# The second expert's two input products as 2x2 blocks by seven products, its gated features kept in float32, and one turned output product

## The chip, the cores and the metric

The kernel runs on one core of a Trainium2 chip. The metric is the device time of one execution in microseconds (us). Four compute engines matter: PE (TensorE: matmuls, with a separate weight-load stream shown as PEld), DVE (VectorE), ACT (ScalarE) and POOL (GpSimd); SP (SyncE) issues the transfers.

## What is computed

```python
def reference(q, k, v, moe_w_in, moe_w_out, moe2_w_a, moe2_w_b, moe2_w_out):
    attn = softmax(causal(q @ k.T / 8)) @ v      # 2 batches, 12 heads, 448 tokens, 64
    x = attn                                     # as 896 tokens x 768
    h = x @ moe_w_in                             # 768 x 2048: the first expert
    y = (h - tanh(h)) @ moe_w_out                # 2048 x 768
    a, b = y @ moe2_w_a, y @ moe2_w_b            # 768 x 1536 each: the second expert
    return (a * b) @ moe2_w_out                  # 1536 x 768
```

## The kernel before

**Precision.** Each float32 operand of a product is split into a high and a low float32r part (names `xh`/`xl`, `wh`/`wl`, `gwh`/`gwl`: a trailing h is the high, l the low part). A product of one 128-deep block is then three matmuls (high by high, high by low, low by high), written by `matmuls` and `product` (lines 208 to 219).

**Weights.** A weight tile is 128 partitions x 768 (six 128x128 blocks; 640 where five are used). Five steps bring it in, each behind the other: `load_part` (two transfers on SP), `magnitude` (ACT, line 150), `bits` (DVE, line 162: tile `t`), `split_high` (ACT, line 173: `wh`) and `split_low` (DVE, line 184: `wl`; POOL during attention). `advance` calls each step once. How far each may run ahead is limited by counters: three raw tiles, TP = 2 tiles `t`, and a ring of seven pairs `wh`, `wl`, whose slots come free as products finish (`at["done"]`).

**Stages.** Attention goes first, in an order written out by hand (`ORDER`), with pieces of the first expert's first group as filler. Then come the three groups of the first expert (5, 6 and 5 feature blocks): `hidden` makes a block's features, and six output products (`dm` 0 to 5) add into `part` in SBUF (line 549); in the last group each sum is split into `yh`, `yl` (called `xh`, `xl` in rows; lines 553 and 554). The second expert has two groups of six feature blocks (`GROUPS2`). A block takes, for each of two pieces of tokens (512 and 384), 18 matmuls by `w_a` and 18 by `w_b`; ACT copies the one result (line 576), DVE multiplies it with the other (line 577), and `halve_g` splits the gated block (lines 466 and 467). After each group come 7 token tiles x 2 halves of an output product, 18 matmuls of 384 columns each; the second group adds to `opart` on DVE (line 599) and stores.

**Order.** Outside attention a scheduler orders each engine's instructions; each engine then works its list strictly in that order. Eight PSUM banks (`s` four, `t` two, `o` and `h` one each) are taken in turn by `next_bank`; a bank holds one product from its first to its last matmul, is read once or twice, and goes to the next product.

## Time and profile before

| | |
|---|---|
| median of 3 runs | 594.86 us (593.68 to 595.03) |
| the profiled execution, time | 593.73 us |
| the profiled execution, span from first to last instruction | 592.0 us |
| PE busy | 584.5 us, 99% of the span |
| DVE busy | 286.8 us, 48% |
| ACT busy | 276.1 us, 47% |
| POOL busy | 75.8 us, 13% |
| HBM read | 61.63 MB |

Busy PE time counts overlapping matmuls, so 99% says only that PE is hardly ever without work. How fast it goes is read from the starts of its matmuls. All durations come from the one profiled execution; its time lies 1.73 us over its span, and the median of the runs lies 1.13 us over its time.

### The profile page before, as it was taken

The numbers are of one execution on the slowest core, as the hardware profiler recorded it, in microseconds if no ns is written. First come the engines' busy times: TensorE is split into PE (matmuls) and PEld (weight loads), VectorE is DVE, ScalarE is ACT, GpSimd is POOL, SyncE is SP. The second block draws the span as 40 slices with busy tenths as digits, with TensorE's granted clock in tenths as the row PEclk, the third lists the DMA queues.
The fourth block names the chain that finished last, engine by engine and source line by source line (L and its number), as shares of the span: only waits on it lengthen the run. The fifth ranks groups of instructions, "written<-read, shape, count | busy, mean of one in ns | idle before, by whom it ended". The sixth has DMA issues, their size and how long they took to land.

```text
span 592.0 us, 8779 instructions
## 1 busy us (share of the span) xinstructions
PE 584.5 (99%) x3386; PEld 519.8 (88%) x3386; DVE 286.8 (48%) x552; ACT 276.1 (47%) x543; POOL 75.8 (13%) x93
## 2 busy tenths in 40 slices
PE   8999999999999999999999999999999999999997
PEld 4777887889988888888988999999999888889997
DVE  5788776427545554445567344444101754442111
ACT  5999888427565542235554333333312753321000
POOL 5788583300000000000000000000000000000000
PEclk9999999999999999999999999999999999999999
DMA  7645442217553332223343333333300843300111
GB/s 224 167 120 157 133 120 90 90 54 221 182 183 107 106 99 90 95 96 111 107 151 107 106 108 106 108 107 106 107 1 0 276 153 115 97 0 2 65 55 66
DMA packets 71114, 64.95 MB, mean 110 GB/s; under 512 B 13984, under 2 KB 71072, under 8 KB 71072
## 3 DMA queue, kind: packets, MB, share of 16 engines
q1 hardware_dynamic: 71072, 64.40, 34.8%
q8 instruction: 26, 0.43, 0.3%
q14 instruction: 16, 0.13, 0.1%
HBM read 61.63 MB, written 2.75 MB: 109 GB/s over the span
## 4 chain that ended last, share of the span: by engine, by line
PE 93%; ACT 5%; DVE 1%; issue 0%; POOL 0%; ACTq 0%; DVEq 0%
PE s L213 42%; PE t L213 19%; PE h L213 13%; PE o L213 9%; ACT p L323 3%; PE o L363 3%; PE t L337 2%; PE s L302 2%; PE h L435 1%; ACT pt L345 1%; PE t L382 0%; DVE p L314 0%; DVE t L162 0%; PE h L337 0%; ACT y L390 0%
## 5 line engine op out<-in xcount | busy, mean ns | idle before, releaser
L150 ACT CAST top<-raw 128x768 f16<-128x768 bf16 (+1 forms) x70 | 73.4, 1049 | 63.6 <-DVE t L162 31.4
L184 DVE TENSOR_TENSOR wl<-t,wh 128x768 fp32r<-128x768 f32 (+1 forms) x63 | 58.8, 936 | 88.3 <-ACT wh L173 86.3
L173 ACT CAST wh<-t 128x768 fp32r<-128x768 f32 (+1 forms) x70 | 56.9, 817 | 79.8 <-PE t L213 32.2
L213 PE MATMUL s<-xh,wl 128*128 128x512 f32 (+2 forms) x222 | 82.7, 373 | 0.0
L213 PE MATMUL s<-xl,wh 128*128 128x512 f32 (+2 forms) x222 | 82.6, 372 | 0.0
L213 PE MATMUL s<-xh,wh 128*128 128x512 f32 (+2 forms) x222 | 82.2, 370 | 0.0
L162 DVE SCALAR_TENSOR_TENSOR t<-raw,top 128x768 int32<-128x768 int32 (+1 forms) x70 | 68.2, 977 | 7.4 <-ACT top L150 5.6
L323 ACT ACTIVATE p<-p,m 112x448 f32<-112x448 f32 (+3 forms) x96 | 49.8, 525 | 6.3 <-DVE m L314 6.3
L213 PEld LDWEIGHTS s<-xl,wh 128*128 128x128 f32 x222 | 41.7, 188 | 5.6
L213 PEld LDWEIGHTS s<-xh,wl 128*128 128x128 f32 x222 | 41.6, 188 | 5.6
L213 PEld LDWEIGHTS s<-xh,wh 128*128 128x128 f32 x222 | 41.7, 188 | 5.6
L314 DVE CUSTOM_DVE_ANT_0 p<-s,mask 112x448 f32<-112x448 f32 (+3 forms) x96 | 37.7, 441 | 7.4 <-PE s L302 6.9
L213 PE MATMUL t<-xh,wl 128*128 128x384 f32 (+2 forms) x114 | 40.3, 354 | 0.0
L213 PE MATMUL t<-xh,wh 128*128 128x384 f32 (+2 forms) x114 | 40.3, 354 | 0.0
L213 PE MATMUL t<-xl,wh 128*128 128x384 f32 (+2 forms) x114 | 40.3, 353 | 0.0
L466 ACT CAST gwh<-e 128x512 fp32r<-128x512 f32 (+1 forms) x24 | 13.5, 563 | 38.8 <-DVE e L577 38.8
L213 PE MATMUL h<-xl,wh 128*128 128x448 f32 (+2 forms) x84 | 31.5, 375 | 0.0
L213 PE MATMUL h<-xh,wh 128*128 128x448 f32 (+2 forms) x84 | 31.3, 372 | 0.0
L213 PE MATMUL h<-xh,wl 128*128 128x448 f32 (+2 forms) x84 | 31.1, 370 | 0.0
L337 PE MATMUL t<-ident,p 112*112 112x112 f32 x202 | 29.6, 265 | 1.2 <-ACT pt L345 0.6
L337 PEld LDWEIGHTS t<-ident,p 112*112 112x112 f32 x202 | 21.3, 133 | 8.2 <-ACT pt L345 2.3
L213 PE MATMUL s<-wh,gwh 128*128 128x384 f32 x84 | 28.1, 334 | 0.0
(144 smaller groups left out, 1241.8 us busy)
## 6 DMA issues: line engine op xcount, KB each, us to landing
raw<-in_moe_w_out SPq DMA_DIRECT2D x48, 383.2 KB, 3.9
raw<-in_moe_w_in SPq DMA_DIRECT2D x32, 383.2 KB, 4.1
raw<-in_moe_w_a SPq DMA_DIRECT2D x24, 383.2 KB, 4.0
raw<-in_moe_w_b SPq DMA_DIRECT2D x24, 383.2 KB, 4.0
raw<-in_moe_w_out SPq DMA_DIRECT2D x12, 255.5 KB, 3.6
qk<-in_q SPq DMA_DIRECT2D x12, 224.0 KB, 2.8
qk<-in_k SPq DMA_DIRECT2D x12, 224.0 KB, 3.7
v<-in_v SPq DMA_DIRECT2D x24, 112.0 KB, 3.0
```

The lines of the kernel that those rows point to most:

```text
L150: nc.scalar.copy(out=tops[i % len(tops)][:, 0:nk, :, 1], in_=top[:, :, :, 2])
L162: nc.vector.scalar_tensor_tensor(out=ts[i], in0=low[:, :, :, 0], scalar=13, in1=top, op0=ALU.logical_shift_right, op1=ALU.bitwise_or)
L173: nc.scalar.copy(out=halves[i][0][:, 0:nk], in_=ts[i].bitcast(F32))
L184: engine.tensor_tensor(out=lo[:, 0:nk], in0=t.bitcast(F32), in1=hi[:, 0:nk].bitcast(F32), op=ALU.subtract)
L213: nc.tensor.matmul(o, a, b_, start=j == 0, stop=j == n - 1)
L302: nc.tensor.matmul(sc[i, c][e], a[r, 0, cs], b_[r, 1, :n], start=x == 0, stop=x == len(terms) - 1)
L314: nc.vector.tensor_tensor_reduce(out=p[:, e], in0=s, in1=mask[:QC, S - n:], scale=-scale, scalar=3.0e38, op0=ALU.add, op1=ALU.min, accum_o ...
L323: nc.scalar.activation(out=p[:, e], in_=p[:, e], func=ACTF.Exp, bias=least[i][:, c, e:e + 1], scale=-1.0, accum_out=sums[i][:, c, e:e + 1],)
L337: nc.tensor.transpose(out=pst[:QC, x * QC:(x + 1) * QC], in_=blk, identity=ident[:QC, :QC])
L345: nc.scalar.copy(out=out_, in_=in_)
L363: nc.tensor.matmul(o[64 * e:64 * e + 64, cs], vt[:, k_, e, :], p.rearrange("s c q -> s (c q)"), start=k_ == 0, stop=k_ == 2 * h + 1, skip_ ...
L466: nc.scalar.copy(out=hi, in_=gg)
```

## The change

The second expert's input products are made in **units**: one unit is one of the two weight matrices by two neighbouring feature blocks, so there are 12. The unit's operands are cut into 2x2 blocks (the 768-deep sum in halves of three blocks; two batches of 448 tokens; two feature blocks), and Strassen's scheme in Winograd's form gives the four results by seven products in place of eight. A product is nine matmuls of 448 columns. Its number m is 1 to 7; `turns` lists (unit, m).

- **Operands.** `y_terms` makes sums and differences of the first expert's output (lines 566 to 589 of the changed kernel) in the last output products, which now go in the order 0, 3, 1, 4, 2, 5 and in two pieces of 448. The extra operands `ext` and `ext4` take slots named `gwh`, `gwl`. `combine` makes four differences of weights for each unit on DVE (lines 188 to 194), in place in `t` or in `s3`. Weights are split half a tile at a time (384 columns), two halves to a ring slot; the ring has five slots instead of seven, `t` four instead of two.
- **Results.** Products 1, 6, 7 and 4 of a unit go one after another into one bank (X), 5 and 3 into a second (Z), 2 into a third (Y). `go_on` lets a product add to what the bank holds after it was read. ACT copies X after 1 and after 6 and Z after 5 (line 690); DVE adds Y to the first copy, X after 7 and Z after 3 to the others (line 664); ACT or DVE reads X once more after 4. DVE multiplies the results of the two matrices into `g32` (line 674).
- **Output.** The gated features stay in float32 until `split_g` splits all 12 blocks (lines 561 and 562), the first during the last unit, the others behind it. The output product then sums over all 12 blocks in one PSUM group: 6 row blocks x pieces of 512 and 384 tokens, 36 matmuls each, weights as the stationary operand; ACT copies the sum (line 725) and it is stored. The output is turned, and the host turns it back.

```diff
-    GROUPS2 = [6, 6]
-    TP = 2
+    DM_ORDER = (0, 3, 1, 4, 2, 5)
+    NF2 = DFF2 // 128
+    TP = 4
+    PARTS = 7
+    WB = 5
...
-    ep = ctx.enter_context(tc.tile_pool(name="e", bufs=2))
+    ep = ctx.enter_context(tc.tile_pool(name="e", bufs=8))
+    s3p = ctx.enter_context(tc.tile_pool(name="s3", bufs=2))
...
+    plan = [(i, None) for i in range(len(tiles))]
+    NU = NF2
+    base = len(tiles)
+    for f in range(0, NF2, 2):
+        for w in (w_a, w_b):
+            tiles += [block(w, slice(0, DM), f), block(w, slice(0, DM), f + 1)]
+    turns = []
+    for u in range(NU):
+        if u == 0:
+            turns += [(0, 1), (0, 5), (1, 1), (1, 5), (0, 2), (0, 6), (0, 7), (0, 3), (1, 2), (0, 4)]
+        elif u == 1:
+            turns += [(1, 6), (1, 7), (1, 3), (2, 1), (1, 4)]
+        elif u < NU - 1:
+            turns += [(u, 2), (u, 6), (u, 5), (u, 7), (u, 3), (u + 1, 1), (u, 4)]
+        else:
+            turns += [(u, 2), (u, 5), (u, 6), (u, 3), (u, 7), (u, 4)]
+    plan += turns
+    for dm in range(KD):
+        for h in range(2):
+            plan.append((len(tiles), None))
+            tiles.append(block(w_o, slice(h * DM, (h + 1) * DM), dm))
...
-        if i >= at["abs"] or i >= at["halve"] + TP:
+        while at["t"] in last_use and last_use[at["t"]] < at["halve"]:
+            at["t"] += 1
+        if i >= at["abs"] or i >= at["t"] + TP:
...
+    def source(j):
+
+        i, m = plan[j]
+        if m is None:
+            return ts[i].bitcast(F32)
+        if m == 7:
+            return thirds[i]
+        t = ts[base + 2 * i + int(m in (4, 5))].bitcast(F32)
+        return t[:, 3:6] if m in (2, 3, 4) else t[:, 0:3]
+
+    def combine(u, m):
+
+        t0, t1 = [ts[base + 2 * u + x].bitcast(F32) for x in range(2)]
+        a11, a12, a21, a22 = t0[:, 0:3], t0[:, 3:6], t1[:, 0:3], t1[:, 3:6]
+        if m == 3:
+            nc.vector.tensor_tensor(out=a12, in0=a12, in1=a11, op=ALU.subtract)
+        elif u not in summed:
+            summed.add(u)
+            thirds[u] = s3p.tile([128, 3, 128], F32, tag="s3", name="s3")
+            nc.vector.tensor_tensor(out=thirds[u], in0=a11, in1=a21, op=ALU.subtract)
+            nc.vector.tensor_tensor(out=a21, in0=a21, in1=a22, op=ALU.add)
+            nc.vector.tensor_tensor(out=a11, in0=a21, in1=a11, op=ALU.subtract)
+
     def split_high():
-        i = at["high"]
-        if i >= at["bits"] or i >= at["done"] + len(w_r.turns):
-            return
-        nk = ts[i].shape[1]
-        halves[i] = w_r.tile([([128, KD, 128], F32R, "wh"), ([128, KD, 128], F32R, "wl")])
-        nc.scalar.copy(out=halves[i][0][:, 0:nk], in_=ts[i].bitcast(F32))
+        j = at["high"]
+        if j >= len(plan) or j > at["halve"]:
+            return
+        i, m = plan[j]
+        full = m is None
+        if (i if full else base + 2 * i + int(m not in (1, 2))) >= at["bits"]:
+            return
+        if full or at["slots"] % 2 == 0:
+            if at["slots"] // 2 >= at["done"] // 2 + WB:
+                return
+            at["pair"] = [w_p.tile([128, KD, 128], F32R, tag=x, name=x) for x in ("wh", "wl")]
+        if m in (3, 5, 6, 7):
+            combine(i, m)
+        x = source(j)
+        nk = x.shape[1]
+        k0 = 0 if full else 3 * (at["slots"] % 2)
+        halves[j] = [t[:, k0:k0 + nk] for t in at["pair"]]
+        at["slots"] += 2 if full else 1
...
+                    o, a, b_, start=j == 0 and not go_on, stop=j == n - 1, skip_group_check=True
...
+    def y_terms(dm, b):
+
+        cs = BATCHES[b]
+        y = part[dm]
+        if b == 0:
+            yh[dm], yl[dm] = [xp.tile([128, NT], F32R, tag=x, name=x) for x in ("xh", "xl")]
+        if dm >= KD // 2 or b == 0:
+            halve(yh[dm][:, cs], yl[dm][:, cs], y[:, cs])
+        if b == 0:
+            return
+        if dm < KD // 2:
+            nc.vector.tensor_tensor(out=y[:, B0], in0=y[:, B1], in1=y[:, B0], op=ALU.subtract)
+            halve(yh[dm][:, B1], yl[dm][:, B1], y[:, B0])
+            return
+        kk = dm - KD // 2
+        t = part[kk]
+        ext[kk] = [g_full[0].tile([128, NT], F32R, tag=x, name=x) for x in ("gwh", "gwl")]
+        nc.vector.tensor_tensor(out=t[:, B0], in0=y[:, B1], in1=t[:, B0], op=ALU.subtract)
+        nc.vector.tensor_tensor(out=t[:, B1], in0=y[:, B1], in1=t[:, B1], op=ALU.subtract)
+        halve(*ext[kk], t)
+        nc.vector.tensor_tensor(out=y[:, B0], in0=y[:, B0], in1=t[:, B0], op=ALU.subtract)
+        if kk % 2 == 0:
+            ext4[kk // 2] = [g_full[0].tile([128, NT], F32R, tag=x, name=x) for x in ("gwh", "gwl")]
+        halve(*[x[:, BATCHES[kk % 2]] for x in ext4[kk // 2]], y[:, B0])
...
-    NTILE = NT // 128
-    NH = DM // 2
...
-            for cs in PIECES:
-                res = []
-                n = cs.stop - cs.start
-                for wh, wl in ws:
-                    o = next_bank()[:, :n]
-                    product(o, [((wh[:, kk], wl[:, kk]), (yh[kk][:, cs], yl[kk][:, cs])) for kk in range(KD)])
-                    res.append(o)
-                aa = ep.tile([128, 512], F32, tag="e0", name="e0")[:, :n]
-                ab = ep.tile([128, 512], F32, tag="e1", name="e1")[:, :n]
-                nc.scalar.copy(out=aa, in_=res[0])
-                nc.vector.tensor_tensor(out=ab, in0=res[1], in1=aa, op=ALU.mult)
-                halve_g(ab, gw[f][0][:, cs], gw[f][1][:, cs])
...
-            for hf in range(2):
-                o = next_bank()[:, :NH]
-                hs = slice(hf * 3, hf * 3 + 3)
-                product(
-                    o,
-                    [((gw[f][0][:, cs], gw[f][1][:, cs]), (ws[f][0][:, hs], ws[f][1][:, hs])) for f in range(g)],
-                )
-                dst = opart[t][:, hf * NH:(hf + 1) * NH]
-                if gi == 0:
-                    nc.scalar.copy(out=dst, in_=o)
-                else:
-                    nc.vector.tensor_tensor(out=dst, in0=o, in1=dst, op=ALU.add)
-                    nc.sync.dma_start(out=out[cs, hf * NH:(hf + 1) * NH], in_=dst)
...
+    def operand(m):
+        out = []
+        for kk in range(NK):
+            if m in (1, 5, 2, 3):
+                t = yh, yl
+                k, b = kk + NK * (m in (2, 3)), m in (5, 3)
+            elif m in (6, 7):
+                t = [{kk: ext[kk][x]} for x in range(2)]
+                k, b = kk, m == 7
+            else:
+                t = [{kk: ext4[kk // 2][x]} for x in range(2)]
+                k, b = kk, kk % 2
+            out.append([x[k][:, BATCHES[b]] for x in t])
+        return out
...
+    def split_g(f):
+
+        pool, tags = (g_full[0], ("gwh", "gwl")) if f == 0 or f > KD else (xp, ("xh", "xl"))
+        gs[f] = [pool.tile([128, NT], F32R, tag=x, name=x) for x in tags]
+        for b, cs in enumerate(BATCHES):
+            halve(*[x[:, cs] for x in gs[f]], g32[f][b])
...
+    def add(x, o):
+        nc.vector.tensor_tensor(out=x, in0=o, in1=x, op=ALU.add)
+
+    def outcome(u, q, x):
+
+        f, b = u // 2 * 2 + q // 2, q % 2
+        if u % 2 == 0:
+            left[q] = x
+            return
+        if f not in g32:
+            new_g32(f)
+        nc.vector.tensor_tensor(out=g32[f][b], in0=x, in1=left.pop(q), op=ALU.mult)
+
+    def turn(u, m):
+
+        wh, wl = next_weights()
+        parts = [((wh[:, kk], wl[:, kk]), b_) for kk, b_ in enumerate(operand(m))]
+        if m == 1:
+            X[u] = next_bank()[:, :S]
+        if m == 2:
+            Y[u] = next_bank()[:, :S]
+        if m == 5:
+            Z[u] = next_bank()[:, :S]
+        o = {1: X, 6: X, 7: X, 4: X, 2: Y, 5: Z, 3: Z}[m][u]
+        product(o, parts, go_on=m in (6, 7, 4, 3))
+        if m in (1, 6, 5):
+            c = {1: c1, 6: c2, 5: z}[m][u] = etile()
+            nc.scalar.copy(out=c, in_=o)
+        elif m == 2:
+            add(c1[u], o)
+            outcome(u, 0, c1.pop(u))
+        elif m == 7:
+            add(z[u], o)
+            outcome(u, 3, z.pop(u))
+        elif m == 3:
+            add(c2[u], o)
+            outcome(u, 1, c2.pop(u))
+        elif u % 2 == 0:
+            c = etile()
+            nc.scalar.copy(out=c, in_=o)
+            outcome(u, 2, c)
+        else:
+            outcome(u, 2, o)
+        at["done"] += 1
+        advance()
+
+    for u, m in turns:
+        if (u, m) == (NU - 1, 2):
+            split_g(0)
+        turn(u, m)
+    for f in range(1, NF2):
+        split_g(f)
+    for dm in range(KD):
+        ws = [next_weights() for _ in range(2)]
+        for cs in PIECES:
+            n = cs.stop - cs.start
+            o = next_bank()[:, :n]
+            product(
+                o,
+                [((ws[f // KD][0][:, f % KD], ws[f // KD][1][:, f % KD]), [x[:, cs] for x in gs[f]]) for f in range(NF2)],
+            )
+            r = ep.tile([128, 512], F32, tag="e", name="e")[:, :n]
+            nc.scalar.copy(out=r, in_=o)
+            nc.sync.dma_start(out=out[dm * 128:(dm + 1) * 128, cs], in_=r)
...
```

How this stands in each engine's list is shown at three places. **PE in the second expert's input stage**, before: the end of one product and the start of the next (`s_3676` and `t_3630` are banks, `xh_`, `xl_` the split output of the first expert, `wh_`, `wl_` weights).

```order
L213 MATMUL t_3630<-xh_3481,wh_3305 128x384
L213 MATMUL t_3630<-xl_3482,wh_3305 128x384
L213 MATMUL t_3630<-xh_3481,wl_3306 128x384
L213 MATMUL t_3630<-xh_3531,wh_3305 128x384
L213 MATMUL t_3630<-xl_3532,wh_3305 128x384
L213 MATMUL t_3630<-xh_3531,wl_3306 128x384
L213 MATMUL s_3676<-xh_3281,wh_3355 128x512
L213 MATMUL s_3676<-xl_3282,wh_3355 128x512
L213 MATMUL s_3676<-xh_3281,wl_3356 128x512
L213 MATMUL s_3676<-xh_3331,wh_3355 128x512
L213 MATMUL s_3676<-xl_3332,wh_3355 128x512
L213 MATMUL s_3676<-xh_3331,wl_3356 128x512
```

The same place now: `s_4103` is bank Z of one unit in its product 5, `h_3917` bank X of the unit ahead, which gets its product 7 here (`gwh_3351` and the like are `ext`).

```order
L251 MATMUL s_4103<-xl_3384,wh_3949 128x448
L251 MATMUL s_4103<-xh_3383,wl_3950 128x448
L251 MATMUL s_4103<-xh_3493,wh_3949 128x448
L251 MATMUL s_4103<-xl_3494,wh_3949 128x448
L251 MATMUL s_4103<-xh_3493,wl_3950 128x448
L251 MATMUL h_3917<-gwh_3351,wh_3852 128x448
L251 MATMUL h_3917<-gwl_3352,wh_3852 128x448
L251 MATMUL h_3917<-gwh_3351,wl_3853 128x448
L251 MATMUL h_3917<-gwh_3463,wh_3852 128x448
L251 MATMUL h_3917<-gwl_3464,wh_3852 128x448
L251 MATMUL h_3917<-gwh_3463,wl_3853 128x448
L251 MATMUL h_3917<-gwh_3566,wh_3852 128x448
```

A bank that was read after product 6 is written again, with another unit's product in between. **DVE in the same stage**, before: `e1` is the gated block, `gwl` its low part, `t` and `wl` the next weights.

```order
L577 TENSOR_TENSOR e1_3605<-h_3585,e0_3604 128x512
L467 TENSOR_TENSOR gwl_3565<-e1_3605,gwh_3564 128x512
L184 TENSOR_TENSOR wl_3656<-t_3509,wh_3655 128x768
L162 SCALAR_TENSOR_TENSOR t_3659<-raw_3461,top1_81 128x768
L577 TENSOR_TENSOR e1_3650<-t_3630,e0_3649 128x384
L184 TENSOR_TENSOR wl_3666<-t_3559,wh_3665 128x768
L162 SCALAR_TENSOR_TENSOR t_3669<-raw_3511,top0_80 128x768
L467 TENSOR_TENSOR gwl_3565<-e1_3650,gwh_3564 128x384
L577 TENSOR_TENSOR e1_3715<-o_3695,e0_3714 128x512
L467 TENSOR_TENSOR gwl_3675<-e1_3715,gwh_3674 128x512
L184 TENSOR_TENSOR wl_3766<-t_3659,wh_3765 128x768
L162 SCALAR_TENSOR_TENSOR t_3769<-raw_3561,top1_81 128x768
```

Now, in steady state (L192, L193, L194 and L188 are `combine`, L224 weight halves, L168 `bits`, L664 the additions, L674 the multiplications):

```order
L192 TENSOR_TENSOR s3_4069<-t_3912,t_3932 128x384
L193 TENSOR_TENSOR t_3932<-t_3932 128x384
L224 TENSOR_TENSOR wl_3984<-s3_3951,wh_3983 128x384
L224 TENSOR_TENSOR wl_3984<-t_3797,wh_3983 128x384
L168 SCALAR_TENSOR_TENSOR t_4031<-raw_3821,top0_83 128x768
L664 TENSOR_TENSOR e_4046<-o_4075,e_4046 128x448
L664 TENSOR_TENSOR e_3997<-h_3917,e_3997 128x448
L224 TENSOR_TENSOR wl_4015<-t_3912,wh_4014 128x384
L674 TENSOR_TENSOR g32_4012<-e_3997,e_3879 128x448
L224 TENSOR_TENSOR wl_4015<-t_3819,wh_4014 128x384
L194 TENSOR_TENSOR t_3912<-t_3932,t_3912 128x384
L664 TENSOR_TENSOR e_3981<-t_3987,e_3981 128x448
```

The instructions are shorter and more of them stand between two readings of a bank. **DVE in the last output products of the first expert**, before: `ypart` is the sum, `xl` its low part.

```order
L549 TENSOR_TENSOR ypart_1995<-s_3264,ypart_1995 128x512
L554 TENSOR_TENSOR xl_3282<-ypart_1995,xh_3281 128x512
L549 TENSOR_TENSOR ypart_1995<-o_3286,ypart_1995 128x384
L184 TENSOR_TENSOR wl_3306<-t_3197,wh_3305 128x768
L554 TENSOR_TENSOR xl_3282<-ypart_1995,xh_3281 128x384
L549 TENSOR_TENSOR ypart_2050<-s_3314,ypart_2050 128x512
L162 SCALAR_TENSOR_TENSOR t_3309<-raw_3137,top1_81 128x768
L554 TENSOR_TENSOR xl_3332<-ypart_2050,xh_3331 128x512
L549 TENSOR_TENSOR ypart_2050<-t_3336,ypart_2050 128x384
L184 TENSOR_TENSOR wl_3356<-t_3259,wh_3355 128x768
L554 TENSOR_TENSOR xl_3332<-ypart_2050,xh_3331 128x384
L162 SCALAR_TENSOR_TENSOR t_3359<-raw_3199,top0_80 128x768
```

The same place now; L577, L583 and L584 are the differences of `y_terms`.

```order
L619 TENSOR_TENSOR ypart_1998<-s_3259,ypart_1998 128x448
L562 TENSOR_TENSOR xl_3277<-ypart_1998,xh_3276 128x448
L619 TENSOR_TENSOR ypart_1998<-o_3281,ypart_1998 128x448
L224 TENSOR_TENSOR wl_3302<-t_3068,wh_3301 128x640
L577 TENSOR_TENSOR ypart_1998<-ypart_1998 128x448
L619 TENSOR_TENSOR ypart_2151<-s_3310,ypart_2151 128x448
L168 SCALAR_TENSOR_TENSOR t_3305<-raw_3132,top1_84 128x768
L562 TENSOR_TENSOR xl_3277<-ypart_1998,xh_3276 128x448
L562 TENSOR_TENSOR xl_3328<-ypart_2151,xh_3327 128x448
L192 TENSOR_TENSOR s3_3438<-t_3254,t_3305 128x384
L619 TENSOR_TENSOR ypart_2151<-t_3332,ypart_2151 128x448
L224 TENSOR_TENSOR wl_3363<-t_3130,wh_3362 128x384
```

Differences, weight differences and weight halves now stand between the additions.

## Rows read from the trace of the kernel before

**Rows 1.** The page: busy time by engine; span in 40 slices, in tenths.

```profile
PE 584.5 (99%) x3386; PEld 519.8 (88%) x3386; DVE 286.8 (48%) x552; ACT 276.1 (47%) x543; POOL 75.8 (13%) x93
...
PE   8999999999999999999999999999999999999997
...
DVE  5788776427545554445567344444101754442111
...
PEclk9999999999999999999999999999999999999999
```

**Rows 2.** The page: the chain that ended last, shares by engine.

```profile
PE 93%; ACT 5%; DVE 1%; issue 0%; POOL 0%; ACTq 0%; DVEq 0%
```

**Rows 3.** Busy time by stage: stretch, us, PE, PEld, DVE, ACT, POOL, clock, DMA, GB/s.

```profile
290.90:327.40 36.50, 36.50 (x182) 32.68 (x181) 24.94 (x36) 17.94 (x25) 0.00 (x0) 1.00 0.39 120
327.40:414.20 86.80, 86.80 (x433) 78.13 (x433) 37.37 (x48) 32.38 (x47) 0.00 (x0) 1.00 0.32 104
414.20:457.90 43.70, 43.70 (x254) 43.70 (x254) 4.49 (x6) 11.10 (x19) 0.00 (x0) 1.00 0.12 37
...
544.70:588.40 43.70, 43.70 (x253) 43.51 (x252) 8.36 (x15) 0.51 (x1) 0.00 (x0) 1.00 0.16 59
588.40:592.00 3.60, 0.13 (x1) 0.00 (x0) 0.56 (x1) 0.00 (x0) 0.00 (x0) 0.94 0.15 55
```

**Rows 4.** Timeline of PE: first matmuls of four stages, and the last (start, duration).

```profile
327.41 0.39 PE L213 MATMUL s<-xh,wh 128*128 128x512 f32 x1
...
414.21 0.33 PE L213 MATMUL s<-wh,gwh 128*128 128x384 f32 x1
...
457.89 0.39 PE L213 MATMUL s<-xh,wh 128*128 128x512 f32 x1
...
544.69 0.33 PE L213 MATMUL s<-wh,gwh 128*128 128x384 f32 x1
...
588.20 0.34 PE L213 MATMUL t<-wh,gwl 128*128 128x384 f32 x1
```

**Rows 5.** Timeline of PE: first and last of 69 matmuls of 448 columns.

```profile
142.08 0.36 PE L213 MATMUL t<-gwl,wh 128*128 128x448 f32 x1
...
155.85 0.37 PE L213 MATMUL s<-gh,wh 128*128 128x448 f32 x1
```

**Rows 6.** Groups by line and shape, DVE: shapes, count | busy us, mean ns | idle before.

```profile
L162 DVE SCALAR_TENSOR_TENSOR t<-raw,top 128x768 int32<-128x768 int32 x58 | 57.5, 992 | 6.5 <-ACT top L150 5.6
...
L184 DVE TENSOR_TENSOR wl<-t,wh 128x768 fp32r<-128x768 f32 x53 | 50.6, 957 | 78.9 <-ACT wh L173 77.0
...
L467 DVE TENSOR_TENSOR gwl<-e,gwh 128x384 fp32r<-128x384 f32 x12 | 6.6, 550 | 0.6 <-ACT gwh L466 0.6
...
L477 DVE TENSOR_TENSOR e<-h,e 128x448 f32<-128x448 f32 x6 | 3.7, 622 | 3.4 <-ACT e L476 3.4
...
L479 DVE TENSOR_TENSOR gwl<-e,gwh 128x448 fp32r<-128x448 f32 x5 | 3.0, 617 | 0.6 <-ACT gwh L478 0.6
```

**Rows 7.** Groups by line and shape, ACT.

```profile
L150 ACT CAST top<-raw 128x768 f16<-128x768 bf16 x58 | 62.4, 1075 | 45.7 <-DMA raw<-in_moe_w_out 17.2 <-DVE t L162 15.3 <-DMA raw<-in_moe_w_a 9.6
...
L466 ACT CAST gwh<-e 128x384 fp32r<-128x384 f32 x12 | 6.1, 506 | 2.7 <-DVE e L577 2.7
...
L547 ACT COPY ypart<-s 128x448 f32<-128x448 f32 x6 | 3.2, 534 | 0.7 <-PE s L213 0.7
...
L478 ACT CAST gwh<-e 128x448 fp32r<-128x448 f32 x5 | 2.8, 569 | 0.0
```

**Rows 8.** Timeline of DVE: two instructions in a row that wait for nothing.

```profile
300.01 0.96 DVE L184 TENSOR_TENSOR wl<-t,wh 128x768 fp32r<-128x768 f32 x1
300.89 0.55 DVE L554 TENSOR_TENSOR xl<-ypart,xh 128x384 fp32r<-128x384 f32 x1
```

**Rows 9.** Timeline: what follows the last matmul.

```profile
588.57 0.56 DVE L599 TENSOR_TENSOR opart<-t,opart 128x384 f32<-128x384 f32 x1 [2.57 <-PE t L213]
589.16 0.33 SPq L600 DMA_DIRECT2D out<-opart  x1
```

More of the change, by code (lines that the diff above doesn't have):

```diff
@@ new lines, in split_high @@
+        if full or at["slots"] % 2 == 0:
[9 more added lines that the diff above has]
+        at["slots"] += 2 if full else 1
+        nc.scalar.copy(out=halves[j][0], in_=x)
@@ L212, in matmuls, with product @@
             for a, b_ in ((ah, bh), (ah, bl), (al, bh)):
-                nc.tensor.matmul(o, a, b_, start=j == 0, stop=j == n - 1)
+                nc.tensor.matmul(
+                    o, a, b_, start=j == 0 and not go_on, stop=j == n - 1, skip_group_check=True
+                )
                 j += 1
                 yield
-    def product(o, parts):
-        for _ in matmuls(o, parts):
+    def product(o, parts, go_on=False):
+        for _ in matmuls(o, parts, go_on):
             pass
@@ L532, in attention_moe_moe2 @@
                     pass
-                at["done"] += cs.stop == NT
+                at["done"] += 2 * (cs.stop == NT)
                 advance()
-        for dm in range(KD):
+        for dm in DM_ORDER if final else range(KD):
             wh, wl = next_weights()
-            for b, cs in enumerate(pieces):
+            for b, cs in enumerate(BATCHES if final else pieces):
                 y = next_bank()[:, :cs.stop - cs.start]
@@ new lines, in attention_moe_moe2, with etile @@
+    X, Y, Z, c1, c2, z, left = {}, {}, {}, {}, {}, {}, {}
+    def etile():
+        return ep.tile([128, 512], F32, tag="e", name="e")[:, :S]
+    def add(x, o):
[8 more added lines that the diff above has]
+        nc.vector.tensor_tensor(out=g32[f][b], in0=x, in1=left.pop(q), op=ALU.mult)
@@ L627 @@
     r = run_bass_kernel_spmd(nc, [arrays], core_ids=[0])
-    return r.results[0]["out"]
+    return np.ascontiguousarray(r.results[0]["out"].T)
```

108 lines of the change are left out of this document (42 added, 66 removed).

## The prediction

> **What bounds the kernel now.** I read the page first: PE is busy for 99% of the span at the full granted clock, DVE for about half [rows 1], and the chain that ended last lies to 93% on PE [rows 2]. A busy PE need not be a fast one, so I looked next at the starts of its matmuls. From 327.41 us, where the second expert begins, to the last start at 588.20, two starts never lie further apart than their size explains, and the stages follow without a gap [rows 4]. So all of the second expert is PE's pace: a matmul saved there is time saved, as long as nothing else becomes late. The stage table shows who could: DVE is busy for 37.4 of 86.8 us in an input stage, ACT for 32.4, and POOL not at all [rows 3].
>
> **Input products on PE.** Before: 12 feature blocks x 2 matrices x 18 matmuls, each once with 512 and once with 384 columns. The two input stages last 414.21 - 327.41 = 86.80 and 544.69 - 457.89 = 86.80 us [rows 4], 173.6 together, which is 0.402 for a pair of 512 and 384. After: 12 units x 7 products x 9 = 756 matmuls of 448 columns. The first expert already has such matmuls in a dense row: 68 distances from 142.08 to 155.85 make 13.77 us, 0.2025 each [rows 5]. That is half of a 512 and 384 pair, so the even cut costs nothing by itself. 756 x 0.2025 = 153.1 us; the change takes off **20.5 us**.
>
> **Output product on PE.** Before: 457.89 - 414.21 = 43.68 us for the first group; for the second, 588.20 plus one distance of 0.17 less 544.69, again 43.68 [rows 4]; together 87.36. After: 6 x 36 = 216 pairs of 512 and 384 at 0.402 = 86.8. It takes off **0.6 us**. The last output products of the first expert go from 512 and 384 to two pieces of 448: 180 x 0.2025 = 36.45 against 36.5 [rows 3], nothing. The sum for PE is **-21.1 us**.
>
> **DVE in the input stage.** A unit now takes PE 63 x 0.2025 = 12.76 us. For it DVE does, at the durations of [rows 6]: two `bits` of 768 (2 x 0.99), four weight differences and seven weight halves of 384 columns (11 x 0.55), three additions from PSUM (3 x 0.62) and on average two multiplications of 448 (2 x 0.62). That is 1.98 + 6.05 + 1.86 + 1.24 = 11.1 us, 87% of PE's time; before it was 43% of the stage [rows 3]. No row shows a difference of two float32 tiles into float32 in SBUF; the halving subtraction of the same width, 0.55, is the nearest, and the 0.62 of an addition that reads PSUM is its upper bound, which makes 11.4. The lower bound is the overlap: an instruction that waits for nothing starts 0.88 us after one of 0.96 [rows 8], so some 0.08 may come off each of 18 instructions, 9.7 us. PE's time is longer at every one of these values, so DVE costs **nothing** by its work alone, with 1.4 to 3.1 us a unit to spare for waits. ACT has two `magnitude` (2 x 1.08), seven halves (7 x 0.51) and three copies or a little more (3.25 x 0.53): 7.5 us of 12.76 [rows 7].
>
> The Trainium skill bears on this (VectorE: DVE Perf Modes, "The DRAIN you can't avoid"): after every instruction the pipe is emptied before the next one goes on, except that one which is not held may start earlier. By the plain rule a unit costs the full 11.1 us, by the overlap that this trace shows 9.7 [rows 8]; by either PE stays behind it.
>
> **DVE at the start of the second expert.** In the last output products of the first expert PE works 36.5 us [rows 3]. DVE's list now holds there, up to the last piece of the operands, 12 additions (7.4 us), 15 halvings of 448 (9.3), three of 896 (1.1 each by the slope between 384 and 768: 3.3), 12 differences (7.4), and weight work (13.7: one whole `wl`, 12 halves, six differences, three `bits`): 41 us by [rows 6]. It cannot end before PE's last sum at 36.5; behind that sum stand 7 us of DVE work until the last low part of `ext`. PE takes that first in product 6 of unit 0, after 53 matmuls of the new stage: 36.5 + 10.7 = 47.2. DVE would be there at 36.5 + 0.6 + 7 = 44, if it isn't late before, and its 34 us ahead of the last sum fit into 36.5 only if the waits for ACT's halves are short. Bounds: 0, and 4.5 us (41 less 36.5, if all that is over comes late). I take **+1**.
>
> **The end of the input stage.** From the addition after product 2 of the last unit, DVE's list has 22 halvings for `split_g` (13.6 us), eight additions and multiplications (5.0), six whole `wl` (5.7) and five `bits` (5.0): 29.3 us by [rows 6]. PE's list has some 160 matmuls there, the last unit's mixed with the first output sums, 33 us. The cover is these output sums, which take blocks as they get ready; should it fail, PE waits for the last blocks. Bounds: 0, and 4 us (DVE late by what it had spare). I take **+1**.
>
> **Smaller items, together 0.** The ring falls from seven slots to five; five slots stay filled while attention ends, so two weight tiles fewer are ready when the first group's output begins, and PE's list now has the remaining feature products there instead. Each of those takes 18 x 0.2025 = 3.6 us and frees a slot, and a tile that waited for it needs at most 2 x 0.51 on ACT and 0.96 on DVE [rows 6, 7], so I expect no wait; bounds 0 and 2. ACT's copy takes DVE's place behind the last matmul [rows 9]: a copy of 448 is 0.53 [rows 7], the addition was 0.56; the store is as large. SP issues the same weight tiles in 153 instead of 173.6 us, so the 104 GB/s of an input stage become 118, which is what the stage ahead of it moves now, 120 [rows 3].
>
> **Sum.** 593.73 (the profiled execution) - 21.1 + 2 = 574.6. The median of the runs lies 1.13 over that execution, so **575.8 us**.
>
> **Rivals.** (a) *Nothing waits*, or the start and end cost less than I put: 593.73 - 21.1 + 1.13 = 573.8. (b) *DVE becomes the pace of the input stage.* For: 87% filled, each weight half waits for ACT's half of the same tile, and in places the difference that ACT needs stands right ahead of the DVE instruction that needs ACT's result; such a place leaves DVE idle for 0.51 and the handing over [rows 7]. Against: the list puts two to five other instructions in between nearly everywhere, and additions that wait for PE wait only while PE is behind. If four of a unit's seven weight halves are exposed so and the pipe overlaps nothing, a unit takes 11.4 + 4 x 0.55 = 13.6, 0.84 over PE's: 12 x 0.84 = 10 us, **584 to 586**. (c) *Start and end cost their upper bounds*: 4.5 + 4 instead of 2, **582**. (d) *The shared bank stops PE.* Before, a bank was read only when its sum was complete and given on in turn; now PE returns to bank X three times and to Z once a unit, each time behind a reader of 0.53 to 0.62 [rows 6, 7]. PE's list has at least 20 matmuls between two turns at one bank, 4 us, so the reader must start more than 3.4 us late before PE stands; behind a PE that stands there, all other products of its list stand too. That can be if DVE or ACT falls behind for good, because a late reader then also delays the weights behind it in the same list. A stop of 0.6 us at all 48 returns would be 29 us: 575.8 + 29 = **605**, slower than before; it is slower from 0.4 us a return on. The Trainium skill states what forces this order (PSUM — Partial Sum Buffer, "PSUM bank collisions raise a hardware error": two engines may not be at one bank at the same time, so the bank must be guarded); no row of this trace shows such a return. (e) That the saving is not there at all would need 448-wide matmuls that cost more than the row says; [rows 5] excludes it.
>
> **How the numbers follow.** My forecast, with (a) as its lower edge, gets 0.72: 573 to 579. (b) 0.13, (c) 0.08, (d) 0.07, of which a fifth would end near the time of before. A measurement of this kernel can tell about 0.3% (1.8 us) from no change. Faster by more: 0.72 + 0.13 + 0.08 = 0.92, less a little for a mixture of (b), (c) and (d): 0.91. Within: 0.02. Slower: 0.07. The range goes from 572.8 (all 21.1 us and a median 1 us nearer to the profiled execution) to 584.5, which takes in (c) and half of (b) and leaves out some 0.15.
>
> **What would show it.** Right: the distances in the input stage are 0.2025 for 756 matmuls, PE's stage from the first unit to the first output sum lasts 153 to 156 us, and DVE is 75 to 90% busy there. Start wrong: a gap on PE at the first product 6, released by DVE's L562. End wrong: gaps between output sums released by ACT or DVE L561 or L562. (b): many short PE gaps released by DVE's weight halves (L224), in every unit. (d): gaps released by L690, L664 or L702 at the first matmul of products 6, 7, 4 or 3. The prediction falls if the gaps of PE behind 327 us sum to more than 10 us.

## The result, and the profile of the changed kernel

The changed kernel takes **579.46 us** (median; 579.10 to 582.26), the kernel before beside it 594.27: a ratio of 0.9761, 95% interval 0.9732 to 0.9790. It saves 14.8 us where 19 were forecast; the time lies 3.7 us over the forecast and within the range. The profile is of the slowest execution, 582.26 us.

The page, with the lines that answer to [rows 1, 2]:

```profile
span 580.6 us, 8654 instructions
...
PE 571.5 (98%) x3206; PEld 498.7 (86%) x3206; DVE 347.6 (60%) x702; ACT 306.2 (53%) x625; POOL 72.8 (13%) x91
...
PE   8999999899999999999999999999999999999997
...
DVE  5787786418425554444559896868787688931000
...
PEclk9999999989999999999999999999999999999999
...
PE 90%; ACT 5%; DVE 1%; DMA 1%; issue 1%; POOL 0%; SPq 0%; ACTq 0%; DVEq 0%
```

New are one slice of PE and one of its clock at 8, around 116 us, and a DVE that is busy for six to nine tenths from 305 to 508 us. Busy time by stage, as in [rows 3]: last output products of the first expert, input stage, its end, output product, tail.

```profile
296.50:333.70 37.20, 37.20 (x182) 33.81 (x181) 29.95 (x53) 16.75 (x29) 0.00 (x0) 1.00 0.17 53
333.70:484.40 150.70, 150.70 (x731) 136.87 (x730) 117.18 (x211) 83.86 (x152) 0.00 (x0) 1.00 0.38 123
484.40:515.00 30.60, 30.60 (x148) 26.91 (x147) 23.97 (x37) 20.84 (x35) 0.00 (x0) 1.00 0.44 142
515.00:577.10 62.10, 62.10 (x314) 56.18 (x312) 5.75 (x6) 8.25 (x13) 0.00 (x0) 1.00 0.10 35
577.10:580.60 3.50, 0.18 (x2) 0.00 (x0) 0.00 (x0) 0.48 (x1) 0.00 (x0) 0.97 0.15 56
```

PE's timeline at the first matmul of the second expert, the first output sum, and the end, with the copy behind it, as in [rows 4, 9]:

```profile
333.71 0.37 PE L251 MATMUL s<-xh,wh 128*128 128x448 f32 x1
...
484.37 0.40 PE L251 MATMUL s<-gwh,wh 128*128 128x512 f32 x1
...
576.94 0.34 PE L251 MATMUL t<-gwh,wl 128*128 128x384 f32 x1
577.36 0.48 ACT L725 COPY e<-t 128x384 f32<-128x384 f32 x1 [5.68 <-PE t L251]
```

The second expert lasts 576.94 + 0.17 - 333.71 = 243.4 us. By the prediction's own terms without a wait it would be 153.1 + 86.8 = 239.9. No wait of PE is recorded in it, so the 3.5 us are in the matmuls: the window of the input stage holds 731 in 150.70 us. Two of these only reach over an edge (a matmul is recorded for 0.37 us but the next starts sooner), and 150.7 / 729 = 0.2067, where [rows 5] gave 0.2025. This time from one matmul's start to the next one's is called the distance below; a dense row is a run of matmuls of one width without a stop. ACT's timeline at the end of attention, and then PE's, show the other loss:

```profile
114.76 0.90 ACT L154 CAST top<-raw 128x640 f16<-128x640 bf16 x1 [1.96 <-DMA raw<-in_moe_w_out]
115.53 0.52 ACT L430 COPY y<-t 128x448 f32<-128x448 f32 x1
```

```profile
113.99 0.37 PE L251 MATMUL h<-xh,wl 128*128 128x448 f32 x1
116.11 0.78 PE L377 MATMUL t<-ident,p 112*112 112x112 f32 x3 [1.76 <-ACT y L430]
```

A `top` on ACT waits for its weights, `y` stands behind it, and PE's last transposes need the bank that `y` empties. PE stands 1.76 us. The kernel before has that wait on ACT too, 1.89 us, and PE does not feel it (its ACT and PE):

```profile
113.60 0.92 ACT L150 CAST top<-raw 128x640 f16<-128x640 bf16 x1 [1.89 <-DMA raw<-in_moe_w_out]
114.38 0.52 ACT L390 COPY y<-t 128x448 f32<-128x448 f32 x1
```

```profile
103.89 2.12 PE L363 MATMUL o<-pt,v 112*64 112x224 f32 x24
...
115.45 0.45 PE L337 MATMUL t<-ident,p 112*112 112x112 f32 x3
```

Counted from the start of these products with `v` (103.89 there, 105.05 in the changed kernel), `top` starts 9.71 us later in both. What differs is PE's list: up to the last transposes it holds twelve matmuls of the first group's output product fewer, some 2.4 us, so PE arrives ahead of `y`.

Behind the wait the granted clock fell to the lower of its levels (1.2 GHz, half) for a while in this execution, 0.56 in the mean of a window of 3.9 us:

```profile
116.10:120.00 3.90, 3.89 (x12) 2.57 (x13) 0.51 (x1) 0.92 (x1) 0.00 (x0) 0.56 0.53 180
120.00:124.00 4.00, 4.00 (x30) 3.31 (x30) 0.00 (x0) 0.00 (x0) 0.00 (x0) 1.00 0.01 4
```

### The profile page after: what moved, and what is told of

It is laid out like the page before. It is cut to its first block, busy times and chain, and to the rows that moved or that the text cites. A ratio compares the mean times of both kernels' runs of the same rounds, so it can differ in the third digit from the quotient of the medians.

```text
span 580.6 us, 8654 instructions
## 1 busy us (share of the span) xinstructions
PE 571.5 (98%) x3206; PEld 498.7 (86%) x3206; DVE 347.6 (60%) x702; ACT 306.2 (53%) x625; POOL 72.8 (13%) x91
## 4 chain that ended last, share of the span: by engine, by line
PE 90%; ACT 5%; DVE 1%; DMA 1%; issue 1%; POOL 0%; SPq 0%; ACTq 0%; DVEq 0%
PE s L251 42%; PE t L251 18%; PE h L251 13%; PE o L251 9%; ACT p L363 3%; PE o L403 3%; PE t L377 2%; PE s L342 2%; DMA qk<-in_q 1%; DVE t L168 1%; ACT pt L385 1%; DMA raw<-in_moe_w_out 1%; DVE p L354 0%; PE t L422 0%; ACT top L154 0%
## 5 line engine op out<-in xcount | busy, mean ns | idle before, releaser
L215 ACT CAST wh<-t 128x384 fp32r<-128x384 f32 (+2 forms) x118 | 70.9, 626 | 92.5 <-PE t L251 38.0
L224 DVE TENSOR_TENSOR wl<-t,wh 128x384 fp32r<-128x384 f32 (+2 forms) x113 | 75.5, 686 | 68.7 <-ACT wh L215 67.9
L251 PE MATMUL s<-xl,wh 128*128 128x512 f32 (+1 forms) x183 | 69.6, 381 | 0.0
L251 PE MATMUL s<-xh,wh 128*128 128x512 f32 (+1 forms) x183 | 69.5, 380 | 0.0
L251 PE MATMUL s<-xh,wl 128*128 128x512 f32 (+1 forms) x183 | 69.5, 381 | 0.0
L168 DVE SCALAR_TENSOR_TENSOR t<-raw,top 128x768 int32<-128x768 int32 (+1 forms) x70 | 68.1, 977 | 1.2 <-ACT top L154 0.5
L251 PE MATMUL s<-gwh,wh 128*128 128x448 f32 (+1 forms) x165 | 62.3, 378 | 0.0
L251 PE MATMUL s<-gwl,wh 128*128 128x448 f32 (+1 forms) x165 | 62.3, 378 | 0.0
L251 PE MATMUL s<-gwh,wl 128*128 128x448 f32 (+1 forms) x165 | 62.3, 378 | 0.0
L251 PE MATMUL t<-xh,wh 128*128 128x384 f32 (+1 forms) x99 | 34.9, 353 | 0.0
L251 PE MATMUL t<-xh,wl 128*128 128x384 f32 (+1 forms) x99 | 34.7, 350 | 0.0
```

Source lines behind the costliest of these rows:

```text
L168: nc.vector.scalar_tensor_tensor(out=ts[i], in0=low[:, :, :, 0], scalar=13, in1=top, op0=ALU.logical_shift_right, op1=ALU.bitwise_or)
L215: nc.scalar.copy(out=halves[j][0], in_=x)
L224: engine.tensor_tensor(out=lo, in0=source(j), in1=hi.bitcast(F32), op=ALU.subtract)
L251: nc.tensor.matmul(o, a, b_, start=j == 0 and not go_on, stop=j == n - 1, skip_group_check=True)
```

## The experiments

Two questions were open: why PE waits at attention's end (the shorter ring, or the order on ACT), and what makes the distance of 448-column matmuls 0.2067 us. A third was put to the term on which the forecast rested most, DVE's spare time.

**1. The changed kernel again**, no edit.

> The changed kernel once more, to see which parts of its profile belong to it and which to one execution. In the profile of the changed kernel 5.5 us are lost up to the first expert's second group against the kernel before: 1.2 from the start of the execution, some 1.9 us of a wait of PE for the copy y (line 430), which stands on ACT behind a top (line 154) that waits for its transfer, and some 2 us at half the granted clock behind that wait. From there on each matmul of 448 columns takes 0.2067 us instead of 0.2025, 3.1 us over 756 of them. Theory 1 (the wait belongs to the order of the kernel): PE waits 1.5 to 2.1 us at the last transposes again, whether the clock falls or not. Theory 2 (0.2067 belongs to the kernel): it is there again. Rival (0.2067 is what a fallen clock leaves behind): 0.2025 wherever the granted clock stays at 1.0 around 116 us, and 0.2067 where it falls. Time 579 to 580 us in the median.

579.24 us (ratio 0.9745, 0.9731 to 0.9760). PE's wait is there again; the clock stays at 1.00 behind it. The rows are that wait in PE's timeline, and windows: behind the wait, and two of dense 448-column matmuls, of the first expert and of the second. The last row is the first expert's window again, in the profile of the result:

```profile
114.85 0.40 PE L377 MATMUL t<-ident,p 112*112 112x112 f32 x2 [1.96 <-ACT y L430]
```

```profile
114.80:118.00 3.20, 3.15 (x16) 2.37 (x17) 0.51 (x1) 0.92 (x1) 0.00 (x0) 1.00 0.77 266
...
135.00:160.00 25.00, 25.00 (x125) 23.15 (x125) 13.13 (x19) 16.91 (x26) 0.00 (x0) 1.00 0.67 218
...
345.00:480.00 135.00, 135.00 (x655) 122.63 (x654) 101.99 (x185) 72.73 (x132) 0.00 (x0) 1.00 0.39 125
```

```profile
135.00:160.00 25.00, 25.00 (x123) 22.71 (x122) 15.53 (x22) 16.66 (x28) 0.00 (x0) 1.00 0.71 231
```

In the second expert 135 / 653 = 0.2067 again, but behind attention the starts lie 0.2027 apart, with the clock at 1.00 in both. So there are two distances, not one, and behind attention the same program shows either: 125 matmuls in the window here, 123 there. They differ in kind as well. In the result's profile every distance from 345 to 480 us is 206 or 207 ns; in the row of [rows 5] they run from 199 to 207 ns, and 0.2025 us is their mean. The wait belongs to the kernel; the fallen clock does not come with it each time. From the end of the wait to the last product with `v` it is 116.11 to 122.66 with the fallen clock and 114.85 to 119.92 without: 1.5 us.

**2. `y` of the last pair on DVE.**

```diff
-                nc.scalar.copy(out=y, in_=ys[i][:, :S])
+                if i == np_ - 1:
+                    nc.vector.tensor_copy(out=y, in_=ys[i][:, :S])
+                else:
+                    nc.scalar.copy(out=y, in_=ys[i][:, :S])
```

> The changed kernel with one copy moved: the y of the last of the twelve head pairs (line 430) is made by DVE instead of ACT, so that it no longer stands behind a top that waits for its transfer. Theory 1 (order, not the number of ring slots by itself): PE's wait of 1.9 us at the last transposes is gone or under 0.5 us, the granted clock stays at 1.0 there, and the time falls by 1.5 to 4 us, to 575.5 to 578. Rival (PE is short of work there in any order, because the ring has two slots fewer): PE waits as long for something else, and the time stays at 579 to 580. If 0.2067 us for a matmul of 448 columns comes from the fallen clock, it is 0.2025 here and the time falls by 3 to 4 us more.

578.49 us (0.9719 to 0.9748). The `top` waits as before (ACT's timeline), and PE does not (window at the same place, and one of the row behind attention):

```profile
114.83 0.92 ACT L154 CAST top<-raw 128x640 f16<-128x640 bf16 x1 [1.95 <-DMA raw<-in_moe_w_out]
```

```profile
114.00:116.00 2.00, 2.00 (x13) 1.25 (x11) 1.32 (x3) 0.92 (x1) 0.00 (x0) 1.00 1.00 298
...
135.00:160.00 25.00, 25.00 (x122) 22.71 (x122) 12.79 (x18) 16.70 (x26) 0.00 (x0) 1.00 0.64 212
```

So PE waits because `y` stands behind `top` on ACT; with `y` elsewhere five slots leave PE enough other work. But the median falls by 0.75 us only, where 1.5 to 4 were expected, and the executions of the two kernels overlap: the row behind attention now runs at 0.2067 (three matmuls fewer in 25 us), some 225 x 0.0040 = 0.9 us. A fallen clock is not needed for 0.2067, since the clock is at 1.00 here.

**3. Six ring slots**: `WB = 6`.

> The changed kernel with six ring slots instead of five. Theory 1 with the ring as its cause: one weight tile more is ready while attention ends, so output products of the first group stand between the last transposes again; the copy y is as late as before but PE has work meanwhile, and the time falls by 1 to 4 us. If only the place of y in ACT's list counts: the wait of 1.5 to 2 us stays, 579 to 580. The second expert should not change by more than 1 us in either case.

580.60 us (0.9736 to 0.9817; four executions from 578.70 to 583.89): no gain that could be told. The twelve output-product matmuls are back in PE's list, but on ACT a second `top` with a wait of its own now stands ahead of `y`, and PE waits as long as in experiment 1 (ACT's timeline, and PE's):

```profile
116.24 0.90 ACT L154 CAST top<-raw 128x640 f16<-128x640 bf16 x1 [1.59 <-DMA raw<-in_moe_w_out]
117.01 0.52 ACT L430 COPY y<-t 128x448 f32<-128x448 f32 x1
```

```profile
117.59 0.50 PE L377 MATMUL t<-ident,p 112*112 112x112 f32 x3 [1.96 <-ACT y L430]
```

**4. The kernel before, cut into 448 and 448.**

```diff
-    PIECES = [slice(a, min(a + 512, NT)) for a in range(0, NT, 512)]
+    PIECES = BATCHES
```

> The kernel before with one edit: all tokens are cut into two pieces of 448 instead of 512 and 384, in the last two groups of the first expert and in both input stages of the second; nothing is computed by fewer products. 1656 matmuls then have 448 columns: 396 in hidden features, 396 in output products, 864 in the second expert's input stages. Theory 2 (a matmul of 448 columns costs 0.2067 in such a stage, against 0.2009 for the mean of 512 and 384): 1656 x 0.0058 = 9.6 us slower, 603 to 605. Rival (0.2025 as in the dense row of the kernel before, and 0.2067 is peculiar to the changed kernel or to one execution): 1656 x 0.0016 = 2.6 us slower, 596 to 598.

598.19 us, 4.1 more than the kernel before beside it (ratio 1.0068, 1.0051 to 1.0085), between the two forecasts, because both distances are in it. Windows of the first expert and of the two input stages:

```profile
180.00:280.00 100.00, 100.00 (x496) 92.75 (x495) 49.72 (x71) 39.93 (x58) 0.00 (x0) 1.00 0.32 102
...
345.00:410.00 65.00, 65.00 (x323) 60.30 (x322) 26.46 (x35) 24.48 (x35) 0.00 (x0) 1.00 0.36 114
460.00:540.00 80.00, 80.00 (x389) 72.69 (x388) 38.32 (x49) 34.99 (x49) 0.00 (x0) 1.00 0.36 119
```

100 / 494 and 65 / 321 are 0.2024 and 0.2025: the first expert and the first input stage. The second input stage is the same code behind an output product of 384-column matmuls, and has 80 / 387 = 0.2067. So the slower distance needs neither Strassen's products nor shared banks.

**5. Only 448 columns up to the first output sum**: experiment 2, and `pieces = BATCHES` for the whole first expert.

> The kernel of the second experiment (y of the last pair on DVE), and the first expert's second and third groups cut into 448 and 448 tokens instead of 512 and 384, so that from the end of attention to the first output sum of the second expert PE sees no other width than 448. Theory A (a dense row of 448-column matmuls keeps the distance it starts with, 0.2027 or 0.2067, until other widths come between): one value from 130 us to 480 us, whichever it has after attention. With 0.2027: 612 more matmuls of 448 cost 612 x (0.2027 - 0.2018) = 0.6 us, 936 behind them save 936 x 0.0040 = 3.7, so 3 us less than the second experiment, 575 to 576. With 0.2067: 612 x 0.0049 = 3.0 us more, 581 to 582. Theory B (the second expert's own stage makes it 0.2067, by its banks or operands): 0.2027 up to the last output products and 0.2067 behind them, 579 to 580.

581.17 us (0.9763 to 0.9798). The row started at 0.2067 and kept it, 135 / 653 again 350 us later. **6. The same with `y` on ACT** as in the changed kernel; the one copy is the only difference.

> The changed kernel, y on ACT as it was, with one edit: the first expert's second and third groups are cut into 448 and 448 tokens, so that PE sees only 448-column matmuls from attention's end to the first output sum of the second expert. It differs from the kernel that ran at 0.2067 us from 125 to 480 us (581.2 us) only in that one copy y, which brings back a wait of PE of 1.96 us at attention's end; in three of four executions with that wait or its place unchanged, the row behind attention ran at 0.2027. If a row keeps the distance with which it starts, and it starts at 0.2027 here: 0.2027 up to 480 us, in the second expert's input products too, and 581.2 + 2.0 - (225 + 612 + 936) x 0.0040 = 576.1 us: faster, although PE waits again. If it starts at 0.2067: 583. If the second expert's own stage sets 0.2067: 0.2027 up to the last output products and 0.2067 behind them, 579 to 580.

576.04 us (0.9672 to 0.9704), as computed, 5.1 us faster than experiment 5 although PE waits 1.82 us again, and although the clock fell behind that wait in the profiled execution. First experiment 5, then 6: a window from the first expert's second group into its third, and one of the second expert:

```profile
180.00:280.00 100.00, 100.00 (x485) 90.87 (x484) 48.20 (x68) 39.32 (x57) 0.00 (x0) 1.00 0.32 103
345.00:480.00 135.00, 135.00 (x655) 122.66 (x654) 102.17 (x186) 71.68 (x130) 0.00 (x0) 1.00 0.40 129
```

```profile
180.00:280.00 100.00, 100.00 (x496) 92.68 (x495) 50.48 (x71) 41.14 (x60) 0.00 (x0) 1.00 0.31 100
345.00:480.00 135.00, 135.00 (x667) 125.13 (x667) 104.39 (x190) 73.95 (x134) 0.00 (x0) 1.00 0.41 129
```

In both the row keeps the distance with which it starts, for 350 us, across stages, banks and operands; theory A holds in both directions here. It is no law: experiment 12 shows a row that changes.

**7. Pieces of 384 and then 512**: experiment 2, and `PIECES = [slice(0, NT - 512), slice(NT - 512, NT)]`.

> The kernel of the second experiment (y of the last pair on DVE), and the two pieces of tokens in the other order, 384 and then 512, in the last two groups of the first expert and in the output product of the second. The dense row of 448-column matmuls then follows a 512-column matmul instead of a 384-column one. If the width just ahead decides which distance the row starts with: 0.2027 instead of 0.2067 from the last output products of the first expert on, 936 x 0.0040 = 3.7 us less, 574.5 to 575.5. If not: 0.2067 again, and 578 to 579 as in the second experiment.

**574.95 us** (0.9653 to 0.9688), 3.5 less than experiment 2. The input stage now has 13 matmuls more in the same 135 us, 135 / 666 = 0.2027 (window, and PE's timeline at the second expert's first and last matmul):

```profile
345.00:480.00 135.00, 135.00 (x668) 125.18 (x667) 106.42 (x193) 76.59 (x138) 0.00 (x0) 1.00 0.40 129
```

```profile
329.12 0.36 PE L251 MATMUL s<-xh,wh 128*128 128x448 f32 x1
...
569.25 0.39 PE L251 MATMUL t<-gwh,wl 128*128 128x512 f32 x1
```

The second expert lasts 569.25 + 0.23 - 329.12 = 240.4 us; the prediction's 239.9 is right within 0.5 us for this distance. **8 and 9** test the reason that I had given, the width just ahead, with one matmul whose result nobody uses: one of 384 columns ahead of the fast row, and one of 512 in the middle of the slow row behind attention (both on top of experiment 7, both sums overwritten).

```diff
+                if final and dm == 0 and b == 0:
+                    nc.tensor.matmul(y[:, :384], wh[:, 0], gw[0][0][:, :384], start=True, stop=True)
...
+                if gi == 0 and dm == 0 and b == 0:
+                    nc.tensor.matmul(y[:, :512], wh[:, 0], xh[0][:, :512], start=True, stop=True)
```

> The kernel with pieces of 384 and then 512 (574.95 us, 0.2027 us for each of the 936 matmuls of 448 columns behind 292 us), and one matmul of 384 columns more, with no use, right ahead of the first of them; its sum is overwritten. If the width just ahead of a dense row decides at which distance the row runs: one matmul of 0.17 us turns 0.2027 into 0.2067 for the whole row, 936 x 0.0040 + 0.17 = 3.9 us more, 578.5 to 579.3. If not: 0.2027, 575 to 575.4.

> The kernel with pieces of 384 and then 512 again, and one matmul of 512 columns more, with no use, in the middle of the row of 448-column matmuls behind attention, which ran at 0.2067 us there from 125 us on; its sum is overwritten by the first output product of the first group. If one wider matmul sets the distance of what follows: 0.2067 ahead of it (some 130 us) and 0.2027 behind it up to the first expert's second group, 150 to 170 x 0.0040 - 0.23 = 0.4 us less, 574.2 to 575. If not: 0.2067 on both sides, and 0.2 us more.

574.29 us (0.9649 to 0.9676) and 575.06 us (0.9655 to 0.9684). Both are misses: the fast row stays fast, the slow one slow, 0.2067 on both sides of the 512 (a window of experiment 8, and one of 9 behind the 512):

```profile
345.00:480.00 135.00, 135.00 (x668) 124.98 (x667) 105.84 (x191) 76.55 (x138) 0.00 (x0) 1.00 0.41 129
```

```profile
135.00:160.00 25.00, 25.00 (x123) 22.71 (x122) 12.63 (x17) 16.32 (x26) 0.00 (x0) 1.00 0.62 205
```

The width of one matmul ahead does not choose. What does is open. A rival is left: in every profile the second expert's row started slow where whole products of 384 columns stand ahead of it and fast where products of 512 do, but no run parts their width from the rest of what the order of the pieces moves, and behind attention the same program was seen at either distance.

**10 and 11. More work for DVE**, four and eight subtractions a unit of a tile of zeros, which nobody reads.

> The changed kernel with four more subtractions of 384 columns on DVE in each of the second expert's 12 units, into a tile that nobody reads: 4 x 0.554 = 2.2 us a unit, 26.6 us in all. DVE has 10.05 us of work in a unit of 63 x 0.2067 = 13.02 us of PE by the profile of the changed kernel, 2.97 to spare. If all of that is usable (the rival of DVE as the pace is far off): no change, 578.5 to 580. If DVE's waits use up 1.5 us of the spare already, 0.7 x 12 = 8.9 us more, 588.

> The same with eight more subtractions a unit: 4.4 us, so that DVE must become the pace. If all of its spare 2.97 us is usable: (4.43 - 2.97) x 12 = 17.5 us more, 596 to 598. If 1.5 us of it are lost in waits: 35 us more, 614. If the next instruction starts before the last one ends, as the trace shows (0.08 us each), less: 12 x 26 x 0.08 = 25 us come off, and it would stay near 580.

602.59 and 629.38 us (one execution each), and neither answers the question: nothing tied the subtractions to the second expert, and they stood in DVE's list during attention, up to 67.5 and 131.6 us. The last products with `v` start at 143.93 us with four, against 119.92 in experiment 1, and the distance in the second expert is 0.2067 as there. They show something else: there the subtractions took longer than the 0.554 us put down for each, 33.8 us in all for four and 71.8 for eight, and cost 23.4 and 50.1 us. **12. Eight subtractions that read the unit's own `wl`**, so that they stay in their stage.

```diff
+        for _ in range(1 + (m == 7)):
+            nc.vector.tensor_tensor(
+                out=scratch, in0=wl.bitcast(F32), in1=wl.bitcast(F32), op=ALU.subtract
+            )
```

> The changed kernel with eight more subtractions of 384 columns on DVE in each of the second expert's 12 units, 4.4 us a unit, which read the low half of the weights of the product just written, so that they cannot be put ahead of that stage (as the other two such kernels' were: their time went into attention). They go to a tile that nobody reads. DVE has 10.05 us of work in a unit of 13.02 us, 2.97 to spare. If all of that is usable: (4.43 - 2.97) x 12 = 17.5 us more than 579.2, 596 to 598. If half of it is lost in waits: 35 us more, 614. If none is usable (DVE's idle time is all in waits that its list needs): 53 us more, 632.

594.43 us (one execution), 15.2 more than experiment 1, for 52.7 us of DVE work (96 x 0.549): nearly all of DVE's spare time is usable. The windows (input stage, its end) and PE's waits between 330 and 510 us:

```profile
345.00:480.00 135.00, 133.69 (x651) 121.55 (x650) 130.92 (x254) 70.50 (x130) 0.00 (x0) 1.00 0.36 116
...
493.50:506.80 13.30, 9.50 (x23) 7.62 (x24) 13.23 (x24) 5.23 (x8) 0.00 (x0) 0.63 0.37 116
```

```profile
PE s L251 <- DVE wl L224: 5.0, 3, 3.7
PE h L251 <- DVE e L664: 3.3, 1, 3.3
PE s L251 <- ACT wh L215: 1.5, 1, 1.5
PE t L251 <- ACT e L690: 0.4, 1, 0.4
```

From 345 to 480 us DVE does 130.92 us of work, where experiment 1 has 101.99, and is 97% busy. PE stands 1.3 us for it: 28.9 us of DVE work in the time of 10.4 units, 2.8 a unit. The rest of the debt is paid at the stage's end, where PE waits longer. The clock falls there too (0.63 in the second window): its matmuls start 0.37 us apart with 448 columns and 0.43 with 512, where 0.20 and 0.23 are usual, an estimated 4 us of the 15.2. Here the distance also changes inside the row: 0.2067 up to 342.7 us, then between 0.202 and 0.203 with no wait of PE at the change (52 / 257 below), and 0.2066 again behind a stop of 0.2 us at 412.5 (25 / 121). Stops of 0.1 us at 358.5 and of 0.8 us at 438.9 change nothing.

```profile
360.00:412.00 52.00, 52.00 (x259) 48.20 (x258) 48.97 (x94) 28.09 (x52) 0.00 (x0) 1.00 0.34 107
414.00:439.00 25.00, 25.00 (x123) 22.61 (x121) 24.86 (x49) 13.34 (x24) 0.00 (x0) 1.00 0.32 100
```

## Why the prediction was right in kind and 3.7 us off

- **Input products, -20.5 us: mis-sized by 3.2.** The step that failed is "the even cut costs nothing by itself". The count of 756 was right and PE stayed the bound, but 0.2025 was read from one dense row of one execution, which was in the faster of two distances. At 0.2067 the products cost 756 x 0.0042 = 3.2 us more. Experiments 5 to 7 show both values for the same products; what chooses between them stays open. The output product came within 0.5 us of what was put.
- **Last output products of the first expert, 0:** 180 matmuls at the same distance, 37.2 us for 36.5 [rows 3], 0.7 more.
- **DVE's work, 0: right.** Its busy share of the input stage is 117.18 / 150.70, 10.1 us in a unit of 13.02, between the two bounds; a float32 difference of 384 columns takes 0.55, as its nearest row said. In experiment 12 DVE takes in 2.8 us a unit more before PE stands, of the 1.4 to 3.1 put down as spare. Groups of DVE in the input stage, by line and shape:

```profile
L664 DVE TENSOR_TENSOR e<-s,e 128x448 f32<-128x448 f32 x18 | 11.0, 623 | 8.1 <-PE s L251 8.1
...
L188 DVE TENSOR_TENSOR t<-t 128x384 f32<-128x384 f32 x11 | 6.1, 555 | 0.0
```

- **Start and end of the second expert, +1 each: 0.** No wait of PE is recorded behind 292 us in experiment 1. At the start DVE works 29.95 of 37.2 us and keeps up.
- **The smaller item of attention's end, "I expect no wait; bounds 0 and 2": 1.96 us.** I weighed how fast a ring slot is filled again, and took the remaining feature products as filler. What went wrong is ahead of that: PE's list lost twelve output-product matmuls there, and a wait on ACT that they covered before reached PE through `y`. Experiment 2 removes it. Experiment 3 shows that the filler of a sixth slot does not, because another `top` then stands ahead of `y`.
- **Sum:** 575.8 + 3.2 + 0.7 + 2.0 - 2 = 579.7, measured 579.5. The kernel before, beside it, was 0.6 us under the forecast's base of 594.86, so some 0.4 us have no account. Misses of both signs partly cancelled: that it is 3.7 us and not 5.7 is luck, since the two waits put at +1 each did not come.
- **Signs and chances.** PE's stage up to the first output sum is 484.37 - 333.71 = 150.7 us, not the 153 to 156 that were named as a sign of being right; the output sums mix with the last unit, as the text on the end of the stage itself says. The chances 0.72 + 0.13 + 0.08 make 0.93, not 0.92; nothing else hangs on that.
- **Rivals.** (b), DVE as the pace, needs some 3 us more work a unit. (d), the shared bank, shows no stop: no wait of PE is recorded behind 285 us in the changed kernel. (e) was excluded by [rows 5] too firmly: part of the saving was indeed missing for the reason it names, a dearer matmul.
- **The better version** is experiment 7, or 8 (574.29 us, intervals overlap): 4.5 to 5.2 us under the changed kernel, by one copy on another engine and two pieces in the other order.

## What to carry to other kernels

Before a wide cut is replaced by an even one, do not price the new width by one dense row. The trace of before had no slower row to read; the cheap test was experiment 4, the even cut alone in the kernel before, whose one profile shows both distances. When an edit takes filler away from PE, go through what the other engines wait for there: a wait that PE did not feel is in the trace of before, with its length, here 1.89 us. Idle time of an engine that works its list in order can be usable nearly to the end: here DVE was filled to 97% over 135 us, and PE stood 1.3 us.
